# Gated linear attention with a feed-forward network: state stored without its zeros, its products on quarters of the TensorE array, y in two banks

## The chip, the cores and the metric

The kernel runs on one core of one Trainium2 chip. The metric is the device time of one execution in microseconds (us), the median of several runs.

## What is computed

For each of 4 batches and 8 heads a state of 48 x 48 numbers runs over 768 tokens, and its output goes through a two-layer feed-forward network (FFN):

```python
for t in range(S):                                    # S = 768
    state = alpha[:, :, t, :, None] * state + einsum('bhd,bhe->bhde', k[:, :, t], v[:, :, t])
    y[:, :, t] = einsum('bhd,bhde->bhe', q[:, :, t], state)
x = y.transpose(0, 2, 1, 3).reshape(4 * 768, 8 * 48)  # 3072 tokens x 384
h = x @ w_in                                          # 384 x 2048
out = maximum(0.01 * h, h) @ w_out                    # 2048 x 384
```

All of it is float32.

## The kernel before, in words

**Attention.** The tokens are cut into chunks of 128 (`C`), six per batch, so there are 24 units (chunk `tb`, batch `b`; the batch runs faster). A unit works on its eight heads as four pairs `p`, with the two heads `s` of a pair on partitions 0 to 47 and 64 to 111 (`HB` = 64, `D` = 48, `BR` = 112); partitions 48 to 63 are a gap. Its steps, in the order of `attention` (L435):

- `scans` (L295): running products of alpha in the chunk on DVE (VectorE), forward (L301) and backward (L307).
- `scaled_q` and `scaled_k` (L321, L329): q and k times these products. Units 0 to 8 are turned by TensorE transposes (L267), later ones by DVE (L276).
- `scores` (L337, products at L343): k by q within the chunk, 48 rows by 128 columns, one head on the upper and one on the lower half of the array's rows, into two banks of PSUM.
- `mask_scores` (L346): the causal mask, by ACT (ScalarE) and POOL (GpSimd), or by DVE for the second head of later units. The scalings of the state that are waiting are issued here (L359, POOL).
- `k_tokens` (L361): k by tokens again (transposes at L366, copy at L368).
- `outputs` (L371): y of the chunk, three groups of products. From the second chunk on, the *state products* (L381): for each pair the whole 112 x 112 matrix `W[0:BR, p, :]`, which holds the two heads' states on its diagonal and zeros elsewhere, times q. Then the eight *value products* (L387): values times masked scores, 128 rows by 48 columns, the two heads of a pair on the two halves of the array's columns. All of them add up in one bank, `y`. Then, except in the last chunk, the eight products of `kv` (L398) into a bank of its own. Last, y is split into a high part (L404, ACT) and a low part (L405, DVE) in `x_sb`.
- `next_state` (L407): state plus kv, for each half of the partitions an addition on DVE (L419; a copy on ACT at L417 in the first chunk) and a scaling left for POOL.

A float32 product is carried out in two passes, each with its own load of weights, and each pass is one record in the profile.

**FFN.** Three units make a block of 384 tokens; there are 8 blocks and 16 slices `f` of `w_in` and `w_out`. Both operands are split into a high and a low part of a rounded type, and three products of the parts are summed: `ffn_in` (L464) issues nine products of 128 x 128 by 384 columns for a slice (L473), ACT and DVE make the activation and split it (L476 to L485), and `ffn_out` (L490) issues nine more (L498), three slices later (`LAG`).

**Order of the work.** Each engine runs its instructions in order; a scheduler in the framework orders them by a model, within limits that the code sets (`issue_after`). First come units 0 to 8 (`AHEAD`), while the weights arrive; the two slices of weights that are converted early and the weight loads are tied to these units by `LOADS`, `STARTS` and `behind`. Blocks 0 and 1 of the FFN follow, with the conversion of the remaining weights. From block 2 on, the steps of units 9 to 23 are threaded between the FFN's slices, about 1.5 steps per slice (2 in block 2). Every product of the FFN uses the whole array.

**PSUM.** `ps_h` holds two banks for `ffn_in` and the warming products, `ps_x` three banks of the kind `a` and three of the kind `b`. Units 0 to 8 take from both kinds in turn; later units take `a` alone (`kinds[:] = "a"`, L543), five banks a unit in a ring of three: two of scores, one of k, one of y, one of kv.

**Start.** Some products on a tile of zeros (`keep_warm`, L157) keep TensorE at work while the first unit's data arrive. `load_weights` (L189) brings `w_in` in an order of rows that matches the order of heads in `x_sb` (`runs`, L184): three of the four pairs give a group of 128 rows each, and the fourth pair's values fill the gaps of the other groups (`gather`, L422). `stepwise` (L604) is another way of computing the same, taken only where the running products leave a safe range; on these data it isn't run.

Of the kernel before, what the change touches and what calls it, by code (L numbers as in the profile page):

```python
# [9 lines left out]
F32 = mybir.dt.float32  # L10
F32R = mybir.dt.float32r
# [4 lines left out]
ALU = mybir.AluOpType  # L16
# [6 lines left out]
def gated_linear_attn_ffn(ctx, tc, q, k, v, alpha, w_in, w_out, out):  # L23
# [49 lines left out]
    def pieces(name, dtype, *shapes):  # L73
# [13 lines left out]
        "small", F32, (P,), (C,), (1,), (2 * NU,), (NP, C), *[(NP, BR)] * B, *[(DM,)] * NV, *[(NP * PITCH,)] * sum(NL)  # L87
# [65 lines left out]
    nc.vector.memset(ones, 1.0)  # L153

    idle = ps_h.tile([P, 512], F32, name="ph")

    def keep_warm(n):  # L157

        for _ in range(n):
            nc.tensor.matmul(idle[:, 0:C], seed[:, 0, :], seed[:, 1, :], start=True, stop=True)  # L160

# [18 lines left out]
    for b in range(B):  # L180
        nc.gpsimd.memset(state[b], 0.0)


    runs = [(0, D, 0, 1, 2 * D), (D, GAP, 6 * D, NG, 1), (HB, D, D, 1, 2 * D), (BR, GAP, 7 * D, NG, 1)]  # L184
# [76 lines left out]
    def transposed(u, i, name, **kw):  # L261

        src = loaded(u, i)
        if u < AHEAD:
            ps = banks4()
            for p in range(NP):
# [3 lines left out]
                if u == 0 and p % 2:  # L270
                    with tc.issue_after(last.ins):
                        keep_warm(2)
# [98 lines left out]
    def outputs(u):  # L371
# [5 lines left out]
        y = banks4()  # L377

        if tb:
            for p in range(NP):  # L380
                nc.tensor.matmul(  # L381
                    y[0:BR, p, :], W[0:BR, p, :], qs[0:BR, p, :], start=p == 0, stop=False, skip_group_check=True
                )
        for p in range(NP):
            for s, lo, m in ((0, 0, D if tb else HB), (1, HB, D)):
                c = (2 * p + s) * D
                nc.tensor.matmul(  # L387
                    y[lo:lo + m, p, :], V[:, c:c + m], masked[u][s][:, p, :],
                    start=not tb and p == 0, stop=p == NP - 1, skip_group_check=True,
                )  # L390
        del masked[u]
        kv = None
        if tb < NC - 1:
            kv = bank()[:, 0:NP * D].rearrange("d (p e) -> d p e", p=NP)
            for p in range(NP):
                for s, lo in ((0, 0), (1, HB)):
                    h = 2 * p + s
                    made["kv", u] = nc.tensor.matmul(  # L398
                        kv[lo:lo + D, p, :], ktok[:, p, lo:lo + D], V[:, h * D:(h + 1) * D], start=True, stop=True
# [3 lines left out]
        xh, xl = (x_sb[0:BR, at:at + NP, n, j * C:(j + 1) * C] for n in (0, 1))  # L403
        made["xh", u] = nc.scalar.copy(xh, y[0:BR])  # L404
        made["x", u] = nc.vector.tensor_tensor(xl, y[0:BR], xh.bitcast(F32), ALU.subtract)  # L405

    def next_state(u):  # L407
# [4 lines left out]
        W = state[b]  # L412
        us = atp.tile([P, NP, D], F32, name="us")
        for lo in (0, HB):
# [305 lines left out]
```

## Time and profile before

| | |
|---|---|
| median of 3 runs | 542.4 us (541.23 to 542.99) |
| profiled execution: span from first to last instruction | 539.2 us (its whole time is not shown apart from the span) |
| TensorE busy in the span | 522.2 us |
| VectorE (DVE), ScalarE (ACT), GpSimd (POOL) busy | 380.5, 233.7, 60.2 us |
| first nine FFN products in a row, start of the steady FFN | 77.05 us |
| state products (L381): start of the first and of the last record | 34.3 and 456.8 us |

In the rows of the profile, PE is the matmul side of TensorE and PEld its loads of weights, which can run beside a product. A row of the groups gives line, engine, operation, output and inputs by the program's names, shape, count, busy time in us, the mean of one in ns, and the idle time of the engine before them with what ended it. The chain of waits is the path that ended last: each piece gives its start and the time that it adds to the path. Matmuls overlap in the array, so a group's time on the chain, and not the sum of its durations, is what it costs. The granted clock (PEclk) is a share of the full clock.

### The profile page before, as it was taken

What the parts mean: (1) busy time and instruction counts of PE and PEld (TensorE: products, weight loads), DVE (VectorE), ACT (ScalarE), POOL (GpSimd) and SP (SyncE); (2) the same over time, 40 slices, a digit from 0 to 9 for tenths busy, and PEclk for the clock granted to TensorE, in tenths of its full rate; (3) what the DMA queues carried; (4) which work ended last, traced back from release to release, by engine and by line L of the source; (5) the groups of instructions that cost most, each with busy time, mean ns of one, the idle gap of its engine ahead of it and who ended that gap; (6) DMA issues with size and microseconds to landing.
All of it is one profiled execution on the core that took longest, in us unless ns stands there. A gap on an engine that the chain in (4) does not pass through costs nothing.

```text
span 539.2 us, 10037 instructions
## 1 busy us (share of the span) xinstructions
PE 522.2 (97%) x3778; PEld 501.8 (93%) x3778; DVE 380.5 (71%) x695; ACT 233.7 (43%) x494; POOL 60.2 (11%) x139
## 2 busy tenths in 40 slices
PE   8889889999999999999999999999999999999995
PEld 8778689999999899999999999999999999999995
DVE  6879999999998897875685775775876534333331
ACT  2755655555543543435334443344343344233332
POOL 4433500000000121110110101001100000000000
PEclk9999999999999999999999999999999999999999
DMA  9999954445723743533332422513301010101001
GB/s 146 166 182 181 198 136 117 118 122 139 190 49 86 197 104 83 106 77 97 75 80 59 119 49 63 104 43 98 70 1 39 1 44 1 23 1 44 1 0 50
DMA packets 92983, 46.64 MB, mean 87 GB/s; under 512 B 57856, under 2 KB 90112, under 8 KB 92928
## 3 DMA queue, kind: packets, MB, share of 16 engines
q1 hardware_dynamic: 92928, 45.93, 38.8%
q8 instruction: 32, 0.52, 0.5%
q14 instruction: 23, 0.19, 0.1%
HBM read 38.83 MB, written 4.72 MB: 81 GB/s over the span
## 4 chain that ended last, share of the span: by engine, by line
PE 87%; DMA 4%; DVE 3%; SPq 1%; issue 1%; ACT 1%; POOL 0%; ACTq 0%; DVEq 0%
PE ph L473 35%; PE b L498 32%; PE a L343 4%; PE a L498 4%; PE a L387 3%; DMA raw<-in_moe_w_in_dram 3%; PE a L381 2%; PE a L366 1%; PE a L398 1%; PE ph L160 1%; PE b L387 1%; PE b L267 1%; DMA small<-in_alpha_dram 1%; SPq L197 1%; DVE pc L301 1%
## 5 line engine op out<-in xcount | busy, mean ns | idle before, releaser
L473 PE MATMUL ph<-large,w 128*128 128x384 f32 x1152 | 226.0, 338 | 3.8 <-DVE t L479 3.8
L473 PEld LDWEIGHTS ph<-large,w 128*128 128x128 f32 x1152 | 200.6, 188 | 6.5 <-DVE t L479 4.8
L498 PE MATMUL b<-w,gh 128*128 128x384 f32 x672 | 169.4, 340 | 0.0
L479 DVE TENSOR_TENSOR t<-ph,t 128x384 f32<-128x384 f32 x128 | 70.4, 550 | 83.9 <-ACT t L476 83.6
L498 PEld LDWEIGHTS b<-w,gh 128*128 128x128 f32 x672 | 119.5, 188 | 2.1 <-ACT gh L481 0.4
L476 ACT ACTIVATE t<-ph 128x384 f32<-128x384 f32 x128 | 62.6, 489 | 135.1 <-PE ph L473 127.2
L481 ACT CAST gh<-t 128x384 fp32r<-128x384 f32 x128 | 65.7, 513 | 111.0 <-DVE t L479 108.6
L498 PE MATMUL b<-w,gl 128*128 128x384 f32 x336 | 107.3, 336 | 0.0
L485 DVE TENSOR_TENSOR gl<-t,gh 128x384 fp32r<-128x384 f32 x128 | 70.4, 550 | 33.4 <-ACT gh L481 29.7
L498 PEld LDWEIGHTS b<-w,gl 128*128 128x128 f32 x336 | 62.5, 188 | 0.1
L354 POOL TENSOR_SCALAR_AFFINE_SELECT sm<-sm 128x512 f32<-128x512 f32 x33 | 21.6, 665 | 121.4 <-ACT sm L353 103.8
L343 PE MATMUL a<-qs,ks 48*128 48x128 f32 x312 | 30.4, 286 | 0.0
L343 PEld LDWEIGHTS a<-qs,ks 48*128 48x128 f32 x312 | 25.4, 188 | 5.3 <-issue 4.7
L359 POOL TENSOR_TENSOR small<-us,pe 48x192 f32<-48x192 f32 x40 | 21.4, 536 | 79.1 <-DVE us L419 70.1
L276 DVE STREAM_TRANSPOSE ks<-small 128x512 f32<-128x512 f32 x15 | 16.7, 1122 | 13.4 <-PE a L366 13.4
L311 POOL COPY pe<-pc 128x4 f32<-128x4 f32 x24 | 5.0, 210 | 184.1 <-DVE pc L301 183.9
L353 ACT COPY sm<-a 128x512 f32<-128x512 f32 x24 | 14.0, 584 | 15.1 <-PE b L343 12.9
L301 DVE TENSOR_TENSOR_SCAN pc<-e,small 128x128 f32<-128x128 f32 x60 | 20.0, 394 | 0.0
L498 PE MATMUL a<-w,gh 128*128 128x384 f32 x96 | 19.7, 336 | 0.0
L307 DVE TENSOR_TENSOR_SCAN rc<-e,small 128x511 f32<-128x511 f32 x15 | 19.1, 1274 | 0.2
L387 PE MATMUL a<-sm,small 128*48 128x128 f32 x256 | 18.1, 278 | 0.3 <-POOL sm L354 0.3
L241 ACT CAST w<-bits 128x768 fp32r<-128x768 f32 x16 | 13.4, 838 | 11.1 <-DVE bits L238 11.0
(84 smaller groups left out, 552.6 us busy)
## 6 DMA issues: line engine op xcount, KB each, us to landing
raw<-in_moe_w_out_dram SPq DMA_DIRECT2D x16, 384.0 KB, 3.6
small<-in_v_dram SPq DMA_DIRECT2D x24, 192.0 KB, 3.9
raw<-in_moe_w_in_dram SPq DMA_DIRECT2D x32, 144.0 KB, 3.9
out_dram<-t SPq DMA_DIRECT2D x24, 192.0 KB, 1.9
small<-in_alpha_dram SPq DMA_DIRECT2D x32, 96.0 KB, 2.3
small<-in_q_dram SPq DMA_DIRECT2D x30, 96.0 KB, 2.4
small<-in_k_dram SPq DMA_DIRECT2D x30, 96.0 KB, 2.3
small<-in_alpha_dram SPq DMA_DIRECT2D x30, 80.0 KB, 2.3
```

Source lines behind the costliest of these rows:

```text
L301: nc.vector.tensor_tensor_scan(pc[:, p, :], aT[:, p, :], ones.broadcast_to([P, C]), 1.0, ALU.mult, ALU.mult)
L307: nc.vector.tensor_tensor_scan(flat[2][:, NP * C - 2::-1], flat[0][:, NP * C - 1:0:-1], flat[1][:, NP * C - 2::-1], last, ALU.mult, ALU.add)
L343: nc.tensor.matmul(ss[s][:, p, :], ks[lo:lo + D, p, :], qs[lo:lo + D, p, :], start=True, stop=True)
L354: nc.gpsimd.affine_select(out=sm[s], in_=sm[s], compare_op=ALU.is_ge, fill=0.0, base=0, pattern=[[0, NP], [1, C]], channel_multiplier=-1)
L359: nc.gpsimd.tensor_tensor(*scalings.pop(0))
L387: nc.tensor.matmul(y[lo:lo + m, p, :], V[:, c:c + m], masked[u][s][:, p, :], start=not tb and p == 0, stop=p == NP - 1, skip_group_check=True,
L473: nc.tensor.matmul(ph, w_in_of(f, wn, g), xt[:, g, :], start=n == 0, stop=n == 3 * NG - 1)
L476: put(ordered, "ACT", lambda: nc.scalar.mul(t, ph, 0.01))
L479: put(ordered, "DVE", lambda: nc.vector.tensor_tensor(t, ph, t, ALU.max))
L481: put(ordered, "ACT", lambda: nc.scalar.copy(gh, t))
L485: made["gl", i, f] = put(ordered, "DVE", lambda: nc.vector.tensor_tensor(gl, t, gh.bitcast(F32), ALU.subtract))
L498: nc.tensor.matmul(po[j], gt[:, js], w_out_of(f, wn), start=f == 0 and n == 0, stop=f == NF - 1 and n == 2)
```

## The change

- The state of a pair keeps its two 48 x 48 matrices below each other, without zeros: `NP * D` columns in place of `NP * BR`. The memsets of the zeros go.
- The state products become eight, one per head, of 48 rows by 48 or 64 columns. A head's row half is `s` as before, its column half `c` is new: pair `p = 2c + n`. Four heads in succession lie on the four quarters of the array. Row half `s` writes bank `y[s]`, so y lies in two banks.
- The value products run in the order n, s, c, and those of `c` = 0 have 64 columns (always, where before only in the first chunk), so that the gap is written.
- kv has no bank of its own: it is written to the free columns of `y[0]`'s bank. Its first half has 64 weight columns in place of 48, so that the state's gap rows hold numbers.
- The split of y into high and low parts is done per bank: two copies and two subtractions of 112 x 256 in place of one each of 112 x 512.
- `next_state` handles all 112 partitions at once: one addition (or copy) and one scaling in place of two each.
- The order of heads in `x_sb` changes (group `g` and half `c` hold head `4c + g`), and with it the rows of `w_in` that `runs` names, and `place` in `stepwise`.
- Behind the last transposes of unit 0, `keep_warm(2)` is replaced by two products on zeros of 512 or 256 columns in the rounded type; the zeros are a new tile with one memset on POOL.

```diff
@@ pieces
-        "small", F32, (P,), (C,), (1,), (2 * NU,), (NP, C), *[(NP, BR)] * B, *[(DM,)] * NV, *[(NP * PITCH,)] * sum(NL)
+        "small", F32, (P,), (C,), (1,), (2 * NU,), (NP, C), *[(NP * D,)] * B, *[(DM,)] * NV, *[(NP * PITCH,)] * sum(NL)
...
+    zeros = cst.tile([P, 4 * C], F32R, name="zeros")
+    nc.gpsimd.memset(zeros.bitcast(F32), 0.0)
...
+    def keep_warm_wide(n):
+
+        for _ in range(2):
+            nc.tensor.matmul(idle[:, 0:n], zeros[:, 0:P], zeros[:, 0:n], start=True, stop=True)
...
-    for b in range(B):
-        nc.gpsimd.memset(state[b], 0.0)
-
-
-    runs = [(0, D, 0, 1, 2 * D), (D, GAP, 6 * D, NG, 1), (HB, D, D, 1, 2 * D), (BR, GAP, 7 * D, NG, 1)]
+
+
+    runs = [(0, D, 0, 1, D), (D, GAP, NG * D, NG, 1), (HB, D, NP * D, 1, D), (BR, GAP, (NP + NG) * D, NG, 1)]
@@ transposed
                 if u == 0 and p % 2:
                     with tc.issue_after(last.ins):
-                        keep_warm(2)
+                        if i == 2:
+                            keep_warm_wide(4 * C if p == 1 else 2 * C)
+                        else:
+                            keep_warm(2)
@@ outputs
-        y = banks4()
-
-        if tb:
-            for p in range(NP):
-                nc.tensor.matmul(
-                    y[0:BR, p, :], W[0:BR, p, :], qs[0:BR, p, :], start=p == 0, stop=False, skip_group_check=True
-                )
-        for p in range(NP):
-            for s, lo, m in ((0, 0, D if tb else HB), (1, HB, D)):
-                c = (2 * p + s) * D
-                nc.tensor.matmul(
-                    y[lo:lo + m, p, :], V[:, c:c + m], masked[u][s][:, p, :],
-                    start=not tb and p == 0, stop=p == NP - 1, skip_group_check=True,
-                )
+        banks = [bank(), bank()]
+        y = [t.rearrange("r (p n) -> r p n", p=NP)[:, 0:2, :] for t in banks]
+
+        def product(p, s, c, lhsT, rhs, **kw):
+
+            nc.tensor.matmul(y[s][HB * c:HB * c + lhsT.shape[-1], p % 2, :], lhsT, rhs, skip_group_check=True, **kw)
+
+        for n in range(2):
+            for c in (0, 1):
+                for s in (0, 1) if tb else ():
+                    p, lo = 2 * c + n, HB * s
+                    m = D if c else HB
+                    product(p, s, c, W[lo:lo + D, p * D:p * D + m], qs[lo:lo + D, p, :], start=n == 0, stop=False)
+        for n in range(2):
+            for s in (0, 1):
+                for c in (0, 1):
+                    p = 2 * c + n
+                    at_v, m = (2 * p + s) * D, D if c else HB
+                    product(p, s, c, V[:, at_v:at_v + m], masked[u][s][:, p, :], start=not tb and n == 0, stop=n == 1)
         del masked[u]
         kv = None
         if tb < NC - 1:
-            kv = bank()[:, 0:NP * D].rearrange("d (p e) -> d p e", p=NP)
+            kv = banks[0][0:BR, 2 * C:2 * C + NP * D]
             for p in range(NP):
-                for s, lo in ((0, 0), (1, HB)):
+                for s, lo, m in ((0, 0, HB), (1, HB, D)):
                     h = 2 * p + s
                     made["kv", u] = nc.tensor.matmul(
-                        kv[lo:lo + D, p, :], ktok[:, p, lo:lo + D], V[:, h * D:(h + 1) * D], start=True, stop=True
+                        kv[lo:lo + m, p * D:(p + 1) * D], ktok[:, p, lo:lo + m], V[:, h * D:(h + 1) * D],
+                        start=True, stop=True, skip_group_check=True,
                     )
         load_values(u + NV)
         live[u] = pe, kv
-        xh, xl = (x_sb[0:BR, at:at + NP, n, j * C:(j + 1) * C] for n in (0, 1))
-        made["xh", u] = nc.scalar.copy(xh, y[0:BR])
-        made["x", u] = nc.vector.tensor_tensor(xl, y[0:BR], xh.bitcast(F32), ALU.subtract)
+        for s in (0, 1):
+            xh, xl = (x_sb[0:BR, at + s:at + s + NG:2, n, j * C:(j + 1) * C] for n in (0, 1))
+            made["xh", u] = nc.scalar.copy(xh, y[s][0:BR])
+            made["x", u] = nc.vector.tensor_tensor(xl, y[s][0:BR], xh.bitcast(F32), ALU.subtract)
@@ next_state
-        W = state[b]
-        us = atp.tile([P, NP, D], F32, name="us")
-        for lo in (0, HB):
-            r = slice(lo, lo + D)
-            if tb == 0:
-                nc.scalar.copy(us[r], kv[r])
-            else:
-                nc.vector.tensor_tensor(us[r], W[r, :, r], kv[r], ALU.add)
-            scalings.append((W[r, :, r], us[r], pe[r].broadcast_to([D, NP, D]), ALU.mult))
+        W = state[b][0:BR]
+        us = atp.tile([P, NP * D], F32, name="us")[0:BR]
+        if tb == 0:
+            nc.scalar.copy(us, kv)
+        else:
+            nc.vector.tensor_tensor(us, W, kv, ALU.add)
+        W, us = (t.rearrange("d (p e) -> d p e", p=NP) for t in (W, us))
+        scalings.append((W, us, pe[0:BR].broadcast_to([BR, NP, D]), ALU.mult))
@@ stepwise
...
```

More of the change, by code (lines that the diff above doesn't have):

```diff
@@ L609, in place @@
         def place(h, e):
-            return (h // 2) * HB + e if h < 2 * NG else e % NG * HB + D + e // NG
+            c, g = divmod(h, NP)
+            return g * P + c * HB + e if g < NG else e % NG * P + c * HB + D + e // NG
         E4 = 4
@@ L629, in stepwise @@
                 aT, qT, kT = T
-                yt = [gps.tile([P, NG, HB], F32, name=f"yt{s}") for s in (0, 1)]
+                yt = [gps.tile([P, DM], F32, name=f"yt{s}") for s in (0, 1)]
                 for p in range(NP):
@@ L653, in stepwise @@
                                 nc.tensor.matmul(
-                                    yt[s].rearrange("t g r -> t (g r)")[:, c:c + 1], st[s * HB:s * HB + D, n, :], ones[s * HB:s * HB + D, :],
+                                    yt[s][:, c:c + 1], st[s * HB:s * HB + D, n, :], ones[s * HB:s * HB + D, :],
                                     start=True, stop=True,
@@ L657, in stepwise @@
                 y = gp.tile([P, DM], F32, name="y", bufs=1)
-                for s in (0, 1):
-                    nc.vector.tensor_copy(y.rearrange("t (g s r) -> t g s r", g=NG, s=2)[:, :, s, :], yt[s])
+                for s, g, r in ((0, slice(0, NG, 2), slice(0, D)), (1, slice(1, NG, 2), slice(0, D)), (1, slice(0, NG), slice(D, HB))):
+                    to, of = (t.rearrange("t (g c r) -> t g c r", g=NG, c=2)[:, g, :, r] for t in (y, yt[s]))
+                    nc.vector.tensor_copy(to, of)
                 xT = gps.tile([P, NG, C], F32, name="gT")
```

## The prediction

> **What bounds the kernel now.** I began with the head of the page, because it says which engine is full: TensorE (PE), 97% of the span.
>
> ```profile
> span 539.2 us, 10037 instructions
> ...
> PE 522.2 (97%) x3778; PEld 501.8 (93%) x3778; DVE 380.5 (71%) x695; ACT 233.7 (43%) x494; POOL 60.2 (11%) x139
> ```
>
> That is an average, so the next view was busy time by stretches (after the window: its length, then PE, PEld, DVE, ACT, POOL, the granted clock, the DMA share and GB/s).
>
> ```profile
> 35.00:45.00 10.00, 7.92 (x81) 7.16 (x79) 5.96 (x13) 6.56 (x15) 3.84 (x8) 0.83 1.12 181
> 55.00:65.00 10.00, 8.51 (x85) 7.17 (x86) 9.91 (x15) 5.49 (x13) 5.00 (x8) 1.00 1.06 239
> 77.00:165.00 88.00, 87.95 (x505) 87.93 (x506) 85.07 (x136) 47.12 (x84) 0.00 (x0) 1.00 0.48 121
> 200.00:300.00 100.00, 100.00 (x764) 96.92 (x764) 74.26 (x141) 40.66 (x93) 11.51 (x27) 1.00 0.36 81
> 300.00:400.00 100.00, 100.00 (x754) 97.21 (x749) 70.03 (x131) 41.41 (x92) 10.54 (x25) 1.00 0.31 73
> 400.00:460.00 60.00, 60.00 (x420) 57.62 (x420) 30.37 (x55) 24.40 (x53) 2.29 (x5) 1.00 0.07 19
> ```
>
> There are three stages. Until 77 us (units 0 to 8 of the attention, no steady FFN) several things are full at once: the DMA share is about 1 or above, DVE reaches 9.91 of 10 us, and PE has holes. From 77 to 165 us only the FFN runs; it has no line of this change. From about 186 to 458 us units 9 to 23 are threaded between FFN products, and from 200 us PE has no hole at all: a microsecond of PE work saved there is a microsecond of time, and one added is one lost. So the change is worth what it does to PE per unit, fifteen times over. For that I read the chain of waits around one unit (start, time on the chain, what).
>
> ```profile
> 318.71 1.56 PE ph L473 x9
> 320.27 0.88 PE a L381 x8
> 321.15 1.01 PE a L387 x16
> 322.16 0.36 PE a L398 x16
> 322.52 1.79 PE b L498 x9
> 324.30 1.56 PE ph L473 x9
> ...
> 328.99 1.09 PE a L343 x16
> 330.09 1.78 PE b L498 x9
> ```
>
> Each float32 product leaves two records, so L381 x8 is the four state products of a unit, L387 x16 the eight value products, L398 x16 the eight of kv, L343 x16 the eight scores. L381 uses the whole array and takes 0.88 / 8 = 0.11 us for each record: that is the pace of one pass over 128 columns. L387 has twice the records and takes about the same, so two run at once, on the two column halves. L343 does it on the two row halves. That two different products run together, and not the two passes of one, is to be seen in the timeline of the first scores, where the two heads' banks have different letters (start, time, instruction):
>
> ```profile
> 10.53 0.37 PE L343 MATMUL a<-qs,ks 48*128 48x128 f32 x1
> 10.53 0.37 PE L343 MATMUL b<-qs,ks 48*128 48x128 f32 x1
> ...
> 10.74 0.27 PE L343 MATMUL a<-qs,ks 48*128 48x128 f32 x1
> 10.75 0.27 PE L343 MATMUL b<-qs,ks 48*128 48x128 f32 x1
> ```
>
> Product b's first pass starts beside a's first, ahead of a's second. So a second pass that waits for its own part of the array does not hold up the product behind it.
>
> Going from one shape of the array to another is paid for. Nine FFN products take 1.56 us, but 1.79 after L398 and 1.78 after L343: 0.22 for leaving halves. Entering: L343 is 1.09 where eight steps of 0.11 make 0.88, so 0.21 into row halves; L387 is 1.01, so 0.13 into column halves.
>
> **The change part by part.** Rows for the small terms:
>
> ```profile
> L343 PEld LDWEIGHTS a<-qs,ks 48*128 48x128 f32 x312 | 25.4, 188 | 5.3 <-issue 4.7 <-ACT sm L353 0.3
> L387 PEld LDWEIGHTS a<-sm,small 128*48 128x48 f32 x256 | 13.5, 123 | 3.0 <-POOL sm L354 0.7 <-DVE qs L276 0.2
> L387 PEld LDWEIGHTS b<-sm,small 128*64 128x64 f32 x32 | 3.3, 137 | 1.0 <-POOL sm L354 1.0
> L405 DVE TENSOR_TENSOR large<-a,large 112x512 fp32r<-112x512 f32 x16 | 11.0, 690 | 0.8 <-ACT large L404 0.5
> L404 ACT CAST large<-a 112x512 fp32r<-112x512 f32 x16 | 9.4, 588 | 6.2 <-PE a L387 6.2
> L419 DVE TENSOR_TENSOR us<-small,a 48x192 f32<-48x192 f32 x30 | 10.4, 345 | 0.5
> L508 ACT COPY t<-b 128x384 f32<-128x384 f32 x21 | 9.5, 480 | 6.1 <-DVE gl L485 3.2 <-PE b L498 2.6 <-DMA out_dram<-t 0.2
> L359 POOL TENSOR_TENSOR small<-us,pe 48x192 f32<-48x192 f32 x40 | 21.4, 536 | 79.1 <-DVE us L419 70.1 <-ACT us L417 7.5
> L181 POOL MEMSET small<- 128x448 f32 x4 | 1.7, 474 | 0.0
> ```
>
> State products. Four whole-array products become eight of 48 rows by 48 or 64 columns, one quarter of the array each, in two rounds of four. Sixteen records; if four run at once that is 4 steps of 0.11, 0.44 us in place of 0.88. No product of the kernel before uses quarters, so the pace is bounded: 0.44 from the pairs of L387 and L343 carried over to both directions, 0.88 if no more than two ever run together. I take 0.44, since rows and columns each allow it and the queue does not block on a second pass.
>
> One more change of shape. Before, L381 needed none (same shape as the FFN) and L387 entered halves. Now the array goes from whole to quarters, quarters to column halves, and back to whole: one entry more. The bounds are 0.13 (L387) and 0.21 (L343), or up to 0.22 if quarters must also be left at the price of halves. The two entries differ chiefly in the weights they load first: 123 ns for 48 columns, 188 for 128. Quarters load 48 or 64 (137 ns), so I take 0.15, near L387. State products: 0.44 + 0.15 - 0.88 = -0.29 us a unit.
>
> Value products. The same eight, sixteen records; each adjacent pair still has the two column halves. Half of them now load 64 columns (14 ns more), under passes of 0.11 us. Nothing; if the loads were uncovered, 8 x 0.014 = +0.11.
>
> kv. The first half now has 64 weight columns, for gap rows. A step here is 0.36 / 8 = 45 ns. By the load rows a column costs (188 - 123) / 80 = 0.8 ns, so a load of 48 takes about 39 ns and one of 64 about 52: if the load sets the step, +13 ns, eight times, +0.10; if the stream does, 0. L343's eight records with 128 columns, which take as long as the pass, do not tell these apart, so I take +0.09, the cautious end.
>
> Net on PE: -0.20 us for each of units 9 to 19 (eleven), -0.29 for units 20 to 23, which have no kv: -2.2 - 1.2 = -3.4 us. Without the kv term and with an entry of 0.13 it is 15 x -0.31 = -4.7; with 0.22 for the entry and 0.10 for kv, 11 x -0.12 - 4 x 0.22 = -2.2.
>
> Bank sharing. y takes two banks at once, and kv the free half of the first, so five banks of a ring of three per unit as before, and the bank of y[0] comes free after the us addition instead of after x. In the chain above that bank's next user, scores (328.99), is 6.5 us behind kv's end (322.52), and the copies and the addition take 0.59 + 0.69 + 0.35: covered. If the cover went, each microsecond of lateness would stop PE at L343. y[1] takes over the bank that held the same unit's second scores, which the value products need read anyway.
>
> x and us. One copy of 512 columns becomes two of 256: ACT by the slope from 480 (384) to 588 (512) about 2 x 372, +0.16; DVE, by the slope from 345 (192) to 690 (512), 2 x 414, +0.14, and one us addition of 345 ns fewer where there is a state, so -0.21. POOL loses a scaling of 536 ns a unit. From 200 us on these engines have room (74.26 of 100), so 0.
>
> First stage. The pieces of it that lie on the chain:
>
> ```profile
> 15.63 0.49 PE a L398 x16
> ...
> 43.84 0.87 PE b L381 x8
> ...
> 54.22 5.84 DMA raw<-in_moe_w_in_dram
> ...
> 69.46 0.36 DVE us L419
> 69.81 0.03 issue
> 69.85 0.56 DVE t L479
> 70.40 0.60 DVE large L405
> ```
>
> kv of units 0 to 3 lies on it (first row): 4 x 0.09 = +0.36; one set of state products: -0.29; near its end one us addition fewer, -0.36, and a longer x, +0.14. Sum -0.15; the rest hangs on weight DMAs, which keep their sizes under the new head order. I take 0. Bounds: -1.0 if DVE alone set the stage (units 4 to 8, 5 x -0.21), and +1.7 if another idle hole brought a second half-clock stretch like the one that holds 35 to 45 us at 0.83 (0.17 x 10). Four memsets of 474 ns leave POOL and one of 512 columns comes; the wide products of zeros stand in for eight narrow passes behind unit 0's last transposes, in a wait for DVE: 0.
>
> Sum: 539.2 - 3.4 = 535.8 of span. The profiled execution's own time is not shown apart from its span; the median of the three runs, 542.4, lies 3.2 above that, so 539.0 us. A measurement of this kernel can tell about 0.3%, 1.6 us, from no change.
>
> **The rivals.** First, pairs only: the array takes two of the small products at once but not four. Then the eight state products cost 0.88, nothing is saved, and the extra entry (0.15) and kv (0.09) remain: 11 x 0.24 + 4 x 0.15 = +3.2, 545.6 us, slower. It decides as soon as L381's successors take over 0.88 - 0.15 = 0.73 us. For it: no row shows four. Against it: halves work in both directions at full pace. Chance 0.12.
>
> Second, strict order of passes: if every pass had to start behind the one issued before it, the two passes of a product, which need the same quarter, would follow each other, and each product would hold up the next: nine steps of 0.11, 0.99 us. That costs 0.99 + 0.15 - 0.88 = +0.26 a unit, with kv 11 x 0.35 + 4 x 0.26 = +4.9, 547.3 us. The rows at 10.53 to 10.75 speak against it: b's first pass starts ahead of a's second. Chance 0.03.
> The Trainium skill, page "TensorE: Matmul & The Clock Gate", section "Part 3: Packing small matmuls — row/col tiling", says that matmuls start and end strictly in program order and only weight loads are pulled ahead. By that rule the time would be this rival's; for the two passes of float32 this case's trace does not agree, as the 10.53 rows show.
>
> Third, no difference: quarters work, but the gain is eaten, by leaving quarters at 0.22 on top of an entry of 0.21 (-0.01 a unit, then kv), or by 1.7 us of clock in the first stage, or because the order of instructions puts FFN products between state and value products, which costs one more entry and exit, 0.35 a unit. Anywhere from 541 to 544. Chance 0.17.
>
> **How the numbers follow.** Four at once with the gain kept: 0.68, 539.0 us, own range 536.8 to 541. Low end of the whole: -4.7 on PE with -1.0 in the first stage, 536.7. High end: the third rival's, 543.5; the first and second lie beyond it with 0.15. Of the forecast's case 0.02 ends within 0.3%, and of the third rival's 0.02 above it: faster 0.66, same 0.17, slower 0.17.
>
> **What would show it.** In the profile of the changed kernel, around one unit from 300 us on: the state products' piece should fall from 0.88 to about 0.59 and hold sixteen records in four clusters; value products stay at 1.0; kv 0.45; the FFN piece behind still 1.79; PE still 100 of 100 in that window. Starts of 0.11 us in pairs mean the first rival, in single file with one overlap the second. A hole in front of the scores with DVE as releaser would mean that bank sharing costs. The first stage should end (first nine FFN products in a row) within a microsecond or so of 77.05. If the state piece shrinks and the time doesn't, I am wrong about the first stage or the clock.

## The result and the profile after

The changed kernel takes 538.85 us (median of 4 runs, 538.5 to 539.03) against 542.69 (541.23 to 543.56), a ratio of 0.9934 with a 95% interval of 0.992 to 0.9949: 3.8 us faster. The profiled execution took 538.77 us for a span of 537.1. All executions of the runs below show this distance between time and span (1.65 to 1.85 us). By it the profiled execution of the kernel before, with its span of 539.2, took about 540.9 (an estimate) and was one of that kernel's quicker ones.

The head of the page:

```profile
span 537.1 us, 10383 instructions
...
PE 518.8 (97%) x3934; PEld 492.6 (92%) x3934; DVE 375.0 (70%) x703; ACT 234.0 (44%) x514; POOL 49.1 (9%) x116
```

PE is busy for 3.4 us less and has still the same share. Of these 3.4, 1.82 lie between the start of the steady FFN and its last slice (448.46 before, 446.64 after) and 1.55 ahead of it, where PE waits for others; that the sum equals the forecast's 3.4 is chance. By stretches (the columns are those of the prediction):

```profile
35.00:45.00 10.00, 8.01 (x102) 6.87 (x100) 6.73 (x15) 6.25 (x15) 3.71 (x8) 0.83 1.22 180
55.00:65.00 10.00, 8.46 (x85) 7.21 (x84) 9.63 (x17) 6.01 (x15) 4.46 (x5) 0.83 0.98 224
200.00:300.00 100.00, 100.00 (x838) 95.11 (x837) 72.42 (x140) 40.91 (x96) 8.61 (x22) 1.00 0.36 83
300.00:400.00 100.00, 100.00 (x764) 95.68 (x763) 68.50 (x132) 41.29 (x96) 7.98 (x20) 1.00 0.30 71
```

From 200 us on PE is full as before: no hole has opened in front of the scores, so bank sharing costs nothing there. In the first stage a second stretch at a lower clock has appeared (0.83 in 55 to 65 us).

The chain of waits around one unit (start, time on the chain, what). L390 now holds the state and the value products, L411 is kv, L351 the scores, L487 and L512 are the FFN:

```profile
317.18 1.56 PE ph L487 x9
318.75 1.60 PE a L390 x27
320.35 0.45 PE a L411 x15
320.80 1.78 PE b L512 x9
...
327.27 1.09 PE a L351 x16
328.36 1.78 PE b L512 x9
```

State and value products together take 1.60 where they took 0.88 + 1.01 = 1.89; kv takes 0.45 instead of 0.36; the FFN behind takes 1.78 as before (1.79). In the timeline of the same unit (start, time, instruction) the sixteen state records are one row, and the value products begin 0.58 us behind their start:

```profile
318.68 0.66 PE L390 MATMUL a<-qs,small 48*64 48x128 f32 x16
319.26 0.32 PE L390 MATMUL a<-sm,small 128*64 128x128 f32 x2
```

The records' own starts lie in four clusters of four, 318.68, 318.84, 318.95 and 319.06, each within 20 ns. The groups of the smaller terms (mean ns of one behind the count and busy time):

```profile
L420 DVE TENSOR_TENSOR large<-a,large 112x256 fp32r<-112x256 f32 x39 | 14.8, 409 | 0.0
L419 ACT CAST large<-a 112x256 fp32r<-112x256 f32 x39 | 13.5, 372 | 8.0 <-PE a L390 7.3
L367 POOL TENSOR_TENSOR small<-us,pe 112x192 f32<-112x192 f32 x20 | 11.9, 594 | 90.2 <-DVE us L432 87.5 <-ACT us L430 2.7
L432 DVE TENSOR_TENSOR us<-small,a 112x192 f32<-112x192 f32 x12 | 4.1, 345 | 0.0
```

The two copies and subtractions for one take 372 and 409 ns each, near the forecast's 372 and 414. An operation of the state on 112 partitions takes on DVE what it took on 48, 345 ns both times, and on POOL a tenth more, 594 against 536. So one of them for two saves about half the work.

The end of the first stage, from the chain:

```profile
55.67 0.86 DVE pw L254
56.53 1.20 DVE rc L315
57.78 1.23 PE b L390 x14
...
75.81 0.56 DVE t L493
76.41 1.83 PE ph L487 x9
```

The steady FFN starts at 76.41 (before 77.05). The chain runs over DVE's work up to 57.78, where PE had been idle for 1.5 us, and again at the end.

**Where the time went.** The starts of the FFN's slices split the two traces at like places. From slice 4 (the start of the steady FFN) to slice 127 the kernel before took 450.32 us, the changed one 448.47: 1.85 gained there. Ahead of slice 4 it gained 0.64 (77.05 against 76.41), and from the start of slice 127 to the end of the span it lost 0.33 (11.85 against 12.18). That makes 2.15, the difference of the two spans. The rest of the 3.8 is not in this pair of traces: the execution of before that was traced was about 1.8 quicker than its median.

The end adds scatter of its own: in all fourteen traces PE is done 6.4 us after the start of slice 127, and the span ends 5.4 to 7.1 us behind that.

### The profile page after: what moved, and what is told of

Read it like the earlier page. It is cut to its first block, busy times and chain, and to the rows that moved or that the text cites. A ratio compares the mean times of both kernels' runs of the same rounds, so it can differ in the third digit from the quotient of the medians.

```text
span 537.1 us, 10383 instructions
## 1 busy us (share of the span) xinstructions
PE 518.8 (97%) x3934; PEld 492.6 (92%) x3934; DVE 375.0 (70%) x703; ACT 234.0 (44%) x514; POOL 49.1 (9%) x116
## 4 chain that ended last, share of the span: by engine, by line
PE 86%; DVE 4%; DMA 3%; issue 2%; ACT 1%; SPq 1%; POOL 1%; ACTq 0%; DVEq 0%; POOLq 0%
PE ph L487 36%; PE b L512 32%; PE a L390 5%; PE a L351 4%; PE a L512 4%; DMA small<-in_alpha_dram 2%; DMA raw<-in_moe_w_in_dram 1%; PE a L374 1%; PE b L272 1%; PE a L411 1%; PE b L390 1%; DVE pc L309 1%; PE b L411 1%; POOL sm L362 1%; DVE rc L315 0%
## 5 line engine op out<-in xcount | busy, mean ns | idle before, releaser
L487 PE MATMUL ph<-large,w 128*128 128x384 f32 x1152 | 227.4, 340 | 2.8 <-DVE t L493 2.8
L487 PEld LDWEIGHTS ph<-large,w 128*128 128x128 f32 x1152 | 201.9, 189 | 5.5 <-DVE t L493 3.9
L512 PE MATMUL b<-w,gh 128*128 128x384 f32 x672 | 170.0, 340 | 0.0
L512 PEld LDWEIGHTS b<-w,gh 128*128 128x128 f32 x672 | 119.7, 188 | 2.2 <-issue 0.5
L512 PE MATMUL b<-w,gl 128*128 128x384 f32 x336 | 107.4, 336 | 0.0
L512 PEld LDWEIGHTS b<-w,gl 128*128 128x128 f32 x336 | 62.5, 188 | 0.1
L362 POOL TENSOR_SCALAR_AFFINE_SELECT sm<-sm 128x512 f32<-128x512 f32 x33 | 22.8, 705 | 113.3 <-ACT sm L361 113.3
L351 PE MATMUL a<-qs,ks 48*128 48x128 f32 x312 | 30.9, 287 | 0.1
L351 PEld LDWEIGHTS a<-qs,ks 48*128 48x128 f32 x312 | 25.9, 189 | 5.4 <-issue 4.4
L390 PE MATMUL a<-sm,small 128*48 128x128 f32 (+1 forms) x312 | 23.2, 282 | 0.1
L367 POOL TENSOR_TENSOR small<-us,pe 112x192 f32<-112x192 f32 x20 | 11.9, 594 | 90.2 <-DVE us L432 87.5
L390 PEld LDWEIGHTS a<-sm,small 128*48 128x48 f32 (+1 forms) x312 | 17.1, 132 | 3.2 <-issue 3.0
L512 PE MATMUL a<-w,gh 128*128 128x384 f32 x96 | 20.0, 336 | 0.0
```

Of the source, the lines that this page charges most:

```text
L351: nc.tensor.matmul(ss[s][:, p, :], ks[lo:lo + D, p, :], qs[lo:lo + D, p, :], start=True, stop=True)
L362: nc.gpsimd.affine_select(out=sm[s], in_=sm[s], compare_op=ALU.is_ge, fill=0.0, base=0, pattern=[[0, NP], [1, C]], channel_multiplier=-1)
L390: nc.tensor.matmul(y[s][HB * c:HB * c + lhsT.shape[-1], p % 2, :], lhsT, rhs, skip_group_check=True, **kw)
L487: nc.tensor.matmul(ph, w_in_of(f, wn, g), xt[:, g, :], start=n == 0, stop=n == 3 * NG - 1)
L512: nc.tensor.matmul(po[j], gt[:, js], w_out_of(f, wn), start=f == 0 and n == 0, stop=f == NF - 1 and n == 2)
```

## The experiments

The kernel before ran beside each, with medians of 541.58, 542.65, 542.59 and 542.14 us in the four sets. In this table e_split and e_kv48 do the state's addition or copy per half again; the other variants of the changed kernel leave it merged. Stretches are those of 3.4 us in which the granted clock was 0.5, counted up to slice 4 (a stretch of 6.8 us counts as two). The columns from the second to the fifth come from each one's profiled execution, which is not its median: that of e_splitscale and of e_narrow was the quickest of twelve, that of e_kvown the slowest.

| kernel | its time, us | first stage ends, us | stretches | slice 4 to 127, us | median of all, us |
|---|---|---|---|---|---|
| changed kernel | 538.77 | 76.41 | 2 | 448.47 | 538.85 |
| changed kernel again | 538.39 | 76.33 | 2 | 448.44 | 539.02 |
| e_byquarter | 541.80 | 78.52 | 3 | 448.43 | 539.84 |
| e_twobytwo | 539.09 | 75.56 | 1 | 448.41 | 539.09 (one run) |
| e_narrow | 538.59 | 75.39 | 1 | 448.42 | 540.92 |
| a_tied | 538.60 | 75.56 | 1 | 448.19 | 539.45 |
| e_splitscale | 537.73 | 75.69 | 0 | 448.43 | 540.02 |
| e_split | 545.89 | 80.54 | 3 | 450.18 (one more stretch inside) | 545.14 |
| e_kv48 | 540.40 | 78.84 | 2 | 448.02 | 541.67 |
| e_kvown | 543.87 | 78.95 | 3 | 449.94 (one more stretch inside) | 541.54 |
| a_warm | 540.54 | 77.36 | 0 | 448.44 | 541.98 |
| before | not shown | 77.05 | 1 | 450.32 | 542.69 |
| before again | 541.82 | 76.40 | 0 | 451.79 (one stretch inside) | 541.82 |
| b_warm | 544.61 | 79.79 | 2 | 450.26 | 544.64 |

**b_again, a_again: both kernels once more,** unchanged, for the scatter.

> The kernel before, once more, to see how its executions differ. The span of its first profile was 539.2 us, 2.1 above that of the changed kernel (537.1), while the medians differ by 3.8. Theory A: the first profile of before was a fast execution; most others lose another 1 to 2 us in the first stage (a second stretch at half clock, or a later start of the steady FFN), so the listed spans lie mostly between 540 and 542 and the whole time is span + 1.7 us, as in the changed kernel. Theory B: before has more time around its span; then the spans cluster at 539 and the whole time is span + 3.

541.82 us (12 runs), ratio 1.0003 (0.9988 to 1.0019), spans of 539.0 to 542.3. Theory A holds as to the distance of 1.7 us and the scatter.

> The changed kernel once more, on the chip and beside the runs that the other kernels of this group share. In its first profile the PE-bound part (slice 4 to slice 127 of the FFN) took 448.5 us against 450.3 before, only 1.8 less, not 3.4; the medians differed by 3.8. Theory A: the steady part gives 1.8 in every execution, and the rest of the 3.8 is the first stage, which differs between executions by stretches at half clock of 3.4 us, 1.3 to 1.7 us each; then the spans of this kernel scatter too, roughly 535.5 to 539, and the difference of the medians is 2 to 4 us. Theory B: the changed kernel has a fixed gain of 3.8 us; then its spans stay at 537 within 0.3 and the difference is 3.8 again less what chance does to the median before.

539.02 us (6 runs), ratio 0.9936 (0.9913 to 0.9959), spans of 536.5 to 538.6. The gain stands, the steady part repeats to 0.03 us, and the spans (536.5 to 538.6) scatter by 2.1, as theory A has it.

**e_byquarter: the four passes of a quarter in succession.**

```diff
-        for n in range(2):
-            for c in (0, 1):
-                for s in (0, 1) if tb else ():
+        for c in (0, 1):
+            for s in (0, 1) if tb else ():
+                for n in range(2):
```

> The changed kernel with the two products of each quarter next to each other (quarter outermost, n innermost) instead of four quarters in succession; nothing else differs. Theory A, a queue that looks only a few products ahead (about four passes that wait, as the 3-3-1-1 order of the last unit's scores suggests): the first quarter's four passes fill it, the quarters overlap only in part, seven steps of 0.11 instead of four: state products 0.58 -> about 0.9 us, no better than the whole-array form, time up by about 15 x 0.33 = 5 us. Theory B, every quarter has a queue of its own that never blocks: order is irrelevant, 0.58 and the time of the changed kernel. Theory C, strictly one after the other in program order: more than 1 us.

539.84 us (10 runs), ratio 0.9957 (0.9937 to 0.9977). The chain around a unit:

```profile
320.70 1.62 PE a L390 x27
322.33 0.45 PE a L411 x15
```

1.62 against 1.60, and the timeline of that unit:

```profile
320.63 0.68 PE L390 MATMUL a<-qs,small 48*64 48x128 f32 x16
321.24 0.32 PE L390 MATMUL a<-sm,small 128*64 128x128 f32 x2
```

The first four records start at 320.635, 320.649, 320.662 and 320.675, one on each quarter, though in the order of the program three more passes of the first quarter stand between the first two. That the program's order reached the array shows in the distances: 13 to 14 ns from quarter to quarter here, where two products stand for each, and 6 to 7 ns in the changed kernel, where one does. So three waiting passes of a quarter do not hold up the other quarters, and the theory of four waiting passes for the whole array fell. What more of them do is not tried here; the scores of unit 23, below, bear on it.

**e_twobytwo: first one column half with both n, then the other** (loops c, n, s).

> The changed kernel with the state products in the order: the two quarters 00 and 11 of the array... that is row half 0 and 1 of the first column half for n = 0 and n = 1, then the two of the second column half. Theory A (four waiting passes): six steps instead of four, state products about 0.8 us. Theory B (no blocking): 0.58 us.

539.09 us (one run). The quarters "00 and 11" of that text are the two row halves of one column half. The piece is 1.62 again: in these three orders, with at most two products of a quarter in a row, the gain does not hang on the order.

**e_kv48: kv's first half with 48 weight columns,** and so addition, copy and scaling of the state again for each half of the partitions, as the gap rows hold no numbers then.

```diff
-                for s, lo, m in ((0, 0, HB), (1, HB, D)):
+                for s, lo, m in ((0, 0, D), (1, HB, D)):
```

> The changed kernel with 48 weight columns in both halves of kv, and with the addition and scaling of the state done per half as before, since the gap rows then hold nothing. Theory A (the load of 64 weight columns sets kv's step): kv falls from 0.45 to 0.36 us a unit, 11 x 0.09 = 1.0 us in the PE-bound part; DVE gets back one addition of 345 ns per unit, which costs nothing there and up to 5 x 0.35 in the first stage, so the time is 0 to 1 us lower. Theory B (kv sharing y's bank sets the step): kv stays at 0.45 and the time is equal or up to 1 us higher.

541.67 us (12 runs), ratio 1.001 (0.9995 to 1.0025): the gain is gone, which neither theory expected. The chain:

```profile
299.98 1.60 PE a L390 x29
301.59 0.36 PE a L411 x16
```

kv is back at 0.36 in the same bank, so the 64 weight columns set its step and not the bank, as the prediction took it, and the slice starts move by -0.09 against the changed kernel at each of units 11 to 19, the forecast's term (around units 9 and 10, where the order differs, +0.4; in all -0.45). What is lost in the trace is lost in the first stage, 78.84 against 76.41 with two stretches each.

**e_split: the state's addition, copy and scaling per half of the partitions, and nothing else.**

```diff
-            nc.vector.tensor_tensor(us, W, kv, ALU.add)
-        W, us = (t.rearrange("d (p e) -> d p e", p=NP) for t in (W, us))
-        scalings.append((W, us, pe[0:BR].broadcast_to([BR, NP, D]), ALU.mult))
+        for lo in (0, HB):
+            r = slice(lo, lo + D)
...
+                nc.vector.tensor_tensor(us[r], W[r], kv[r], ALU.add)
+            Wr, ur = (t[r].rearrange("d (p e) -> d p e", p=NP) for t in (W, us))
+            scalings.append((Wr, ur, pe[r].broadcast_to([D, NP, D]), ALU.mult))
```

> The changed kernel with the addition (or copy) and the scaling of the state done per half of the partitions, as before; kv keeps its 64 weight columns and its place. In the earlier run with 48 columns this edit came along, and its steady FFN started at 78.84 us instead of 76.4, its time was that of the kernel before. Theory A: the one addition, copy and scaling fewer per unit is what the first stage gains, because DVE, ACT and POOL lie on its path; then the steady FFN starts 1 to 3 us later, the PE-bound part from slice 4 to slice 127 stays at 448.4 us, and the time is 541 to 542 beside 542.5 before. Theory B: the start of the steady FFN is a matter of the clock and of DMAs alone; then the time is that of the changed kernel, ratio 0.993 to before.

545.14 us (12 runs), ratio 1.0044 (1.003 to 1.0058): slower than the kernel before, and 6 us slower than the changed one. Its chain at the places of the first stage shown above:

```profile
51.70 0.51 POOL small L367
52.28 0.52 POOL small L367
52.86 0.65 POOL sm L362
...
58.88 1.20 DVE rc L315
60.12 1.27 PE b L390 x14
...
74.74 0.37 DVE us L434
```

The products of y that began at 57.78 begin at 60.12, and the stage ends at 80.54; the direction is theory A's, the size more than any theory gave. Two scalings lie one behind the other on POOL ahead of the mask (L362), and the second additions lie on DVE. One more run told these apart.

**e_splitscale: the scaling alone per half,** the addition merged.

```diff
-        scalings.append((W, us, pe[0:BR].broadcast_to([BR, NP, D]), ALU.mult))
+        for r in (slice(0, HB), slice(HB, BR)):
+            scalings.append((W[r], us[r], pe[r].broadcast_to([r.stop - r.start, NP, D]), ALU.mult))
```

> The changed kernel with one thing undone in part: the scaling of the state is issued per row half again (64 and 48 partitions, two POOL operations a unit instead of one), while the addition or copy stays merged for all 112 partitions. Undoing both, addition and scaling, had cost 6 us in the medians and made the first stage end at 80.54 instead of 76.41 us. Theory A: the two scalings in succession on POOL, ahead of the mask on the same engine, carry the loss; then this kernel ends its first stage at 79 us or later and takes 543 to 546 us. Theory B: the second addition or copy on DVE and ACT carries it; then this kernel stays within 0.3% of the changed kernel, 538 to 540.5 us, with a first stage that ends at 75.4 to 77. Theory C: both add up; 540.5 to 543.

540.02 us (12 runs), ratio 0.9958 (0.9941 to 0.9975). Its chain:

```profile
43.29 0.51 POOL small L367
43.87 0.52 POOL small L367
44.45 0.65 POOL sm L362
...
57.31 0.34 DVE us L432
...
75.08 0.56 DVE t L494
75.69 1.83 PE ph L488 x9
```

The two scalings are on the chain here too, and yet the stage ends at 75.69. That trace is of the quickest of the twelve executions, but the median too lies where theory B has it. Theory A fell: the loss of e_split needs the second addition or copy. (The addition alone per half was not tried, so the two may also need each other.)

**e_narrow: `keep_warm(2)` in place of the wide products of zeros,** and no tile of zeros.

```diff
-                        if i == 2:
-                            keep_warm_wide(4 * C if p == 1 else 2 * C)
-                        else:
-                            keep_warm(2)
+                        keep_warm(2)
```

> The changed kernel with the narrow warming products of before behind unit 0's last transposes, and without the tile of zeros. Theory A: these products lie in a wait for DVE and the next cause of a half-clock stretch comes 25 us later, so the time is that of the changed kernel within 0.3%. Theory B: the wide products are what keeps the clock up in the first stage; without them one more half-clock stretch, 1.3 to 1.7 us more.

540.92 us (12 runs), ratio 0.9968 (0.995 to 0.9985), whose interval overlaps that of a_again. The medians speak for the wide products by 1.9 us, half of the whole gain; the profiled execution, the quickest of the twelve, speaks against them (75.39 for the first stage). Not settled.

**a_warm, b_warm: products of zeros into the holes,** in the changed kernel and in the one before, meant to keep the clock up; their results are not used. The core of a_warm's edit is shown. At unit 5, index 2, a_warm has five such products ahead of the transposes and b_warm five behind them; both have four more in an output bank of the FFN:

```diff
+    FILL = {(8, 2): 5}
+                if p == NP - 1 and (u, i) in FILL:
+                    with tc.issue_after(last.ins):
+                        for _ in range(FILL[u, i]):
+                            nc.tensor.matmul(idle, zeros[:, 0:P], zeros, start=True, stop=True)
```

> The changed kernel with products on zeros (results unused) put into the holes of TensorE in the first stage: five of 512 columns before the third transposes of unit 5 (the hole at 35 us), five behind those of unit 8 (the hole at 56 us), and four into an output bank of the FFN before its first use (the hole at 75 us). Theory A (half-clock stretches follow holes, and cost 1.3 us each where PE is on the path): no half clock between 8 us and the end of the FFN, the first nine steady FFN products start at about 75 instead of 76.4 us, spans 535 to 536 with less scatter. Theory B (the clock doesn't matter because DVE and DMA set the first stage): same time as the changed kernel or 0.5 to 1 us more, for the added products.

> The kernel before with the same products on zeros, behind the third transposes of units 5 and 8 and ahead of the first use of an output bank. Theory A: spans fall to about 538 with less scatter, and the difference to the changed kernel with the same filling is the PE-bound part's 1.8 us and at most 1 us of the first stage. Theory B: no effect on the time; then the scatter of before has another cause than the clock.

a_warm: 541.98 us (12 runs), ratio 0.9977 (0.9952 to 1.0001). By stretches:

```profile
35.00:45.00 10.00, 7.75 (x109) 6.64 (x109) 5.66 (x13) 6.13 (x15) 2.88 (x7) 1.00 1.13 174
55.00:65.00 10.00, 9.15 (x99) 7.62 (x98) 9.90 (x20) 6.40 (x15) 4.56 (x6) 1.00 1.02 224
```

The clock is 1.00 in both where the changed kernel has 0.83, and yet the first stage ends 0.95 us later than there, DVE at 9.90 of 10, and the median is 3.0 above the changed kernel's beside it (539.02), more than either theory gave. The products at unit 5 didn't fill the hole: 34.98 to 37.25 is still empty, and they lie on the chain behind it with 1.15 us (37.90, PE ph L276 x5). So this run cannot tell the worth of the clock from the price of the filling. b_warm took 544.64 us, ratio 1.0041 (1.0024 to 1.0058), against both of its theories, and its clock did not stay up (two stretches, at 38.18 and 68.90). Filling the holes in this way does not pay; whether the clock bounds this stage stays open.

**a_tied: the unit's products tied behind the last FFN product,** so that fewer FFN products come between them; the second bank's state products first.

```diff
+            with behind("pe") if u >= AHEAD else nullcontext():
+                made["pe",] = nc.tensor.matmul(
...
-                for s in (0, 1) if tb else ():
+                for s in (1, 0) if tb else ():
```

> The changed kernel with the state and value products of units 9 to 23 put in one row behind the FFN product that was issued last, starting with the second bank, so that the scheduler can't put an FFN slice between them. In the changed kernel it does so at units 9 and 20. Theory A (such a split costs two more changes of shape, about 0.33 us each, where the whole-array form of before paid nothing): the PE-bound part falls from 448.4 to 447.8 to 448.1 us, the time by 0.3 to 0.6 us, which the median may not show. Theory B (FFN products between them are free): 448.4, as the changed kernel.

539.45 us (7 runs), ratio 0.9943 (0.9922 to 0.9963). The steady part is 0.28 shorter than the changed kernel's, which lies between the theories. The split at unit 20, told of below, is gone and with it 0.56; unit 9 is still split, after its first product, and around it 0.3 is lost. The time cannot be told from the changed kernel's.

**e_kvown: kv in a bank of its own.**

```diff
-            kv = banks[0][0:BR, 2 * C:2 * C + NP * D]
+            kv = bank()[0:BR, 0:NP * D]
```

> The changed kernel with kv in a bank of its own: six banks a unit in the ring of three instead of five. Theory A (a covered wait): the PE-bound part stays at 448.4 us and kv's piece at 0.45, since the load of 64 columns sets it; the first stage, where banks are short, may lose up to 1 us. Theory B (kv in y's bank delays the copies of y and so the next scores): the PE-bound part gets shorter, by up to 0.3 us a unit.

541.54 us (12 runs), ratio 0.9983 (0.9964 to 1.0003), 2.5 slower than the changed kernel where theory A had up to 1. As theory A has it, kv's piece stays at 0.45, and the steady part is longer by 1.5, at the stretch of low clock inside it (1.47 for the one in before again). So sharing the bank costs nothing there. The traced loss lies in the first stage and in stretches of low clock, which differ between executions; that a lack of banks is what opens its 3.2 us hole at 33.7 was argued, not shown. A sixth bank a unit brings no gain.

## Why the prediction came out

The forecast was 3.4 us less; it is 3.8. That the totals agree is in part luck: the steady part gave 1.85 and not the 3.4 that were to come from it alone, and what it lacked came from the first stage, taken as 0, and from what the medians hold beyond the traced pair.

**Price of a unit: right.** State products 0.29 less forecast: 1.60 for state and value products is 0.59 + 1.01, the forecast's numbers. kv 0.45 as forecast, confirmed by e_kv48's 0.36. Net -0.20 forecast for a unit with kv: the slice starts of the two traces differ by a step of -0.19 at each of units 10 to 19, and by -0.28, -0.29 and -0.26 at units 21, 22 and 23 (-0.29 forecast). Pairs only (0.73 or more for the state products) and strict order (0.99) are ruled out by the 0.58 between the two groups.

The Trainium skill, page "TensorE: Matmul & The Clock Gate", section "Part 3: Packing small matmuls — row/col tiling", has matmuls start and end strictly in program order. For two-pass float32 products on different quarters the trace does not agree: with e_byquarter's order the rule would let a quarter start only with the last of the four passes ahead of it, three steps of 0.11 us later, and four quarters start within 40 ns.

**"Net ... eleven ... four": the count failed.** The steady part gained 1.85, not 3.4, because three places gave time back: 0.45, 0.55 and 0.33, 1.3 of the missing 1.55. The chain at unit 9:

```profile
185.33 1.16 PE a L390 x14
186.49 1.76 PE ph L487 x9
188.24 1.16 PE a L390 x14
```

Here the scheduler put nine FFN products between the products of the two banks, that is of the two row halves, so only two quarters work at a time and the array enters and leaves its parts twice: 2.32 in place of 1.60. The kernel before was split here too, within its value products (0.35 at 186.92, nine FFN products, 0.84 at 189.03), so the difference of the traces moves by +0.25 only, instead of -0.20. At unit 20:

```profile
398.43 0.36 PE a L390 x2
398.79 1.76 PE ph L487 x9
400.55 1.60 PE a L390 x28
```

The two records of one state product come ahead of nine FFN products. They take 0.36, two passes and an entry, and the FFN behind them 1.76 in place of 1.56, the exit; the other fourteen records still take the four steps. That is 0.56 for the split, of which about 0.35 are the entry and exit that the third rival names, and the slice starts move by +0.26 instead of -0.29. The kernel before had the same split:

```profile
400.68 0.22 PE a L381 x2
400.90 1.56 PE ph L473 x9
402.47 0.66 PE a L381 x6
```

There 0.22 + 0.66 is the 0.88 of the whole, and the FFN's 1.56 holds no exit: it cost nothing. That was the hidden cost of leaving the FFN's shape. At unit 23:

```profile
446.08 1.42 PE a L351 x16
447.50 1.78 PE b L512 x9
```

The scores take 1.42 instead of 1.09. They are issued as three of one row half, three of the other, then one and one, and not in turn. The first half's three products make six passes. The second half's first record starts at 446.339, with the third of the six (446.333), when three of them still wait. In e_byquarter three passes of a quarter wait and hold up nothing. Both fit one rule, that up to three passes of a part can wait without holding up what stands behind them; no run tried it by itself, so it is not shown. The third rival's mechanism was real; it struck 2 units of 15.

**"I take 0" for the first stage: too small a gain.** The traces give -0.7 in the profiled executions (76.41 against 77.05), -1.5 to -1.7 with one stretch of low clock on each side (75.39 to 75.56 in e_narrow, e_twobytwo and a_tied), and -0.7 with none (75.69 in e_splitscale against 76.40). The lower bound, -1.0 "if DVE alone set the stage", was nearer. e_split shows the cause in part: per half, units 4 to 8 have five more additions (5 x 0.345 = 1.7 us on DVE) and units 0 to 3 four more copies on ACT (4 x 0.31 = 1.2). The stage grows by 2.0 against e_byquarter (three stretches each), and by 2.4 in e_kv48 against the changed kernel (two each), about that work itself. So without the merged addition the change would have gained nothing or lost (ratio 1.001 in e_kv48, 1.0044 in e_split), which no term of my sum said. Of e_split's 6 us the rest lies partly in one more stretch of low clock behind its hole at 78 to 80.5 (half of 3.4 us; 450.18 against 448.4 for slice 4 to 127), and is not accounted for in full. What the change's merging is worth against the copies in two parts that came with it (409 x 2 for 690 ns on DVE) was not measured apart.

The last hole of the stage got shorter too: PE idles for 1.97 and 1.95 us ahead of the steady FFN in the two traces of the kernel before, for 0.95 and 0.96 in the two of the changed one. In before again that hole brought a stretch of low clock into the steady part, at 77.35, which cost 1.47 (451.79 against 450.32). The changed kernel may be spared such stretches, and its medians may gain by that; two traces of each don't show how often.

**"+1.7 us" for a second stretch of low clock: it came, and cost less.** The changed kernel's trace has two:

```profile
38.00:39.00 1.00, 1.00 (x22) 0.66 (x15) 0.52 (x1) 1.00 (x5) 0.87 (x2) 1.00 1.29 106
39.00:43.00 4.00, 4.00 (x48) 3.84 (x48) 3.67 (x10) 1.47 (x6) 0.37 (x2) 0.57 1.26 165
43.00:46.00 3.00, 3.00 (x42) 2.44 (x40) 1.65 (x4) 2.74 (x7) 1.73 (x3) 1.00 1.12 193
```

Two stretches against one go with 76.3 to 76.4 against 75.4 to 75.6, 0.9 us for one; none at all (e_splitscale) goes with 75.69. These are different kernels, so 0.9 is no more than a sign. In this stage PE waits for others, so slower passes can fall into waits.

**The span's distance to the time** was taken as 3.2, as the profiled execution's own time was not known. It is 1.7; by that the other 1.5 was that execution's luck. Both kernels were carried over alike, so the forecast did not suffer.

Open: which way the remaining 2 us of the medians divides between merged addition, shorter state products, wide zeros (taken as 0; e_narrow's medians would give them 1.9) and low clock; and what holds up the scores at unit 23.

## What to carry to other kernels

Small products that are packed onto parts of the array gain per group, but each place where an order splits the group pays for entering and leaving the shape again, and for passes that run without neighbours (0.56 at unit 20 here): count the splits in the trace of before, those that cost nothing there included. Where an engine other than TensorE sets a stage, look for operations whose time does not depend on the partitions and merge them. A total that comes out right proves no term of its sum; check each against its own stretch of the trace.

## What was not expected of the hardware

- Four float32 products on the four quarters run at the pace of one: sixteen passes start in four clusters, 0.16 us apart at first and then 0.11, and in three orders of issue the piece takes 1.60 to 1.62.
- The low clock comes behind smaller holes than I thought, and on a grid. The stretch at 39.1 follows the hole from 35.1 to 37.1 (2.0 us), the one at 59.6 that from 56.3 to 57.8 (1.5 us). In all fourteen traces the granted clock changes only at whole multiples of 3.413 us from where it is first full (4.97 in the changed kernel). Of the windows so cut ahead of the last product, 20 have PE idle for 1.5 us or more, and 18 of them bring on low clock; of all others only three do, with 1.45, 1.15 and 1.14. All traces have a hole at about 35 to 37 us; in eight, 1.45 us of idling or more falls into one window and low clock follows, in six the grid cuts the hole so that no window has over 1.26, and none follows. So the number of stretches hangs on where the grid falls in an execution as well as on the kernel. The Trainium skill, page "TensorE: Matmul & The Clock Gate", section "Part 1: The HAM clock gate (the "warmup" mystery)", names a window of 3.4 us; the length of the stretches agrees with it.
- A kv product's step goes with the number of its weight columns: 0.45 us for eight steps when half of the loads have 64 columns, 0.36 with 48, or 56 against 45 ns for a step. That the load is what takes this time fits the load rows and is not shown apart.
